# Scheduling a transformer block's instruction queues with the timeline simulator, through an inner tile context

## The chip, the cores and the metric

The kernel runs on one core of a Trainium2 chip. The metric is the device time of one execution in microseconds (us), as the slowest core shows it; a median over several executions is quoted with its range.

The profile of this kernel shows five queues of instructions that run side by side (their busy times in the kernel before add up to 1612.7 us in a span of 740.6 us) and wait for each other by semaphores (the longest wait of TensorE there, for VectorE, took 2.6 us): TensorE (PE in the profile; PEld is its weight load), VectorE (DVE), ScalarE (ACT), GpSimd (POOL) and the sync engine (SP), which here issues nearly all transfers (298 of 322). Each queue has an order, and it counts: in copy_late, one of the runs below, one copy stands five places further back on VectorE, and TensorE waited 2.4 us for it. The text of a kernel does not fix these orders: a scheduler in the tile layer does when the program is built, except where the kernel asks for program order.

## The reference, cut to what matters

```python
def _A_ref(x, wqkv, wo):                     # x: 1 x 2048 x 1024 in bf16, 32 heads of 32
    q, k, v = split(x @ wqkv)
    phi = lambda t: jnp.where(t > 0, t + 1, jnp.exp(t)) + 1e-6
    pq, pk = phi(q), phi(k)
    kv = jnp.einsum("bhsd,bhse->bhde", pk, v);  z = jnp.einsum("bhsd->bhd", pk)
    num = jnp.einsum("bhqd,bhde->bhqe", pq, kv)
    den = jnp.einsum("bhqd,bhd->bhq", pq, z)[..., None] + 1e-6
    return merge_heads(num / den) @ wo
def _B_ref(x, W_gate, W_up, W_down):          # 1024 -> 3584 -> 1024
    gate = x @ W_gate;  gate = gate * (gate > 0)
    return (gate * (x @ W_up)) @ W_down
h = x + _A_ref(_layernorm(x), wqkv, wo)
h2 = h + _B_ref(_layernorm(h), W_gate, W_up, W_down)
```

## The kernel before

The large products are done with Strassen's scheme: seven products of half size (tags A, D, E) instead of eight, and sums of inputs and of weights on VectorE. In time the kernel is: a start (layer norm of the first tiles, transposition on TensorE, plain K and V products), Strassen products for K and V, Strassen products for Q, the attention output in 16 tiles of 128 tokens, an early part of the gated MLP, then the MLP, where the kernel itself fixes the order of TensorE, VectorE and ScalarE, and the down projection.

*The start.* A token tile is transposed on TensorE into a PSUM tile `tp`, of which there is one buffer (`bufs=1`). So TensorE can't begin the next four transposes before the copy out of `tp` is done (in the trace of after, one copy ended at 26.67 us and the transposes behind it began at 26.73), on VectorE for the first half of a tile and on ScalarE for the second.

```python
        def ln_T(t):                                            # cut
            for k in range(2):
                nc.vector.bn_stats(out=stats[:, k, :], in_=x_sb[:, k * NW:(k + 1) * NW])      # L256
            nc.vector.bn_aggr(out=mv[:], in_=stats[:])                                        # L258
            ...
        def transpose_in(t, xn):
            s, i, r = place(t)
            for k in range(2):
                pt = pspool.tile([P, KH, P], BF16, tag="D", bufs=1, name="tp")
                for kc in range(KH):
                    nc.tensor.transpose(pt[:, kc, :], xn[:, (k * KH + kc) * P:(k * KH + kc + 1) * P], ident[:])   # L283
                (nc.scalar.copy if k else nc.vector.tensor_copy)(                             # L284
                    out=xT[s][i][:, k * KH:(k + 1) * KH, r:r + P], in_=pt[:])
```

*The attention output.* A tile goes through a chain: products `nd` on TensorE (L511), logarithm and exponential on ScalarE (L515, L517), a multiplication on VectorE (`o_sb`, L518), a transposing transfer (`oT`, L525), the output product on TensorE (`attn`, L541, 16 matmuls), the residual sum on VectorE (`x_res`, L543). `nd` and `attn` share three PSUM buffers. The kernel traces half of the 224 Q products (L438) among the first tiles, and the early MLP products (L705) among the later ones.

```python
    rest = [p for s in range(1, NS) for c in range(0, KH, 2) for p in [q_unit(s, c)] * 6]
    for step in range(QSTEPS):
        now = rest[step * len(rest) // QSTEPS:(step + 1) * len(rest) // QSTEPS]
        ...
        attn_step(step)
        ...
        for p in now:
            next(p)
```

*The loads of the down projection's weights*, in the MLP, on the sync queue. Sums of W_down (`wt`) are stored to `t_dram` through the same queue.

```python
            if k == nwin - 3:
                for x in range(2):
                    t = wpools[1].tile([P, KC * 2 * GP * P], BF16, tag=("wg", "wu")[x], name="wd")
                    wtiles[x] = t[:, 0:FQ * DW].rearrange("p (f d) -> p f d", f=FQ)
                    load_w(0, x)                                # L837, 896 KB each
```

## Time and profile before

| | before |
|---|---|
| time, median | 744.03 us (743.5 to 746.0, 3 runs) |
| span of the profiled run | 740.6 us |
| TensorE busy, granted clock | 721.8 us, 1.00 |

The first lines are the page's parts 1 and 2: busy time by engine, and the span in 40 equal slices, where a digit is the busy share, or for PEclk the granted clock, in tenths (9 is 90% or more).

```profile
span 740.6 us, 10570 instructions
PE 721.8 (97%) x3967; PEld 382.0 (52%) x4020; DVE 563.2 (76%) x991; ACT 322.0 (43%) x580; POOL 5.7 (1%) x44
...
PE   7999999999989999999999999999999999999997
...
PEclk9999999999999999999999999999999999999999
```

TensorE is what bounds this kernel: 18.8 us of the span without it busy is all there is to win by order.

The same by stretches of time (windows view of before; columns: window, length, then busy us of PE, PEld, DVE, ACT, POOL with instructions in brackets, PEclk as a fraction, DMA share, GB/s).

```profile
core 0: us, PE busy (x) PEld busy (x) DVE busy (x) ACT busy (x) POOL busy (x), PEclk, DMA share, GB/s
20.00:40.00 20.00, 19.89 (x98) 9.28 (x99) 19.45 (x48) 16.11 (x33) 0.00 (x0) 1.00 0.74 154
...
190.00:260.00 70.00, 65.62 (x346) 31.38 (x351) 57.48 (x153) 50.10 (x137) 0.31 (x1) 1.00 0.74 170
```

In the attention stretch TensorE has 4.4 us of idle time in 70.

What TensorE waited for (waits view of before: engine, what waited, what released it; us in total, times, longest), first the longest in 0 to 60 us, then those of 1 us and more in 180 to 260 us:

```profile
PE tp L283 <- DVE xT L284: 2.6, 1, 2.6
```

```profile
PE Eq L705 <- DVE hs L117: 2.0, 1, 2.0
PE Aq L438 <- ACT u L154: 1.1, 1, 1.1
PE nd L511 <- DVE o_sb L518: 1.0, 2, 0.8
```

The order can be read from TensorE's timeline of before in the attention stretch (start, us, then the group of matmuls, and in square brackets the idle time just before it):

```profile
186.28 1.46 PE L438 MATMUL Aq<-xT,tq 128*128 128x512 bf16 x5 [1.10 <-ACT u L154]
187.57 3.62 PE L541 MATMUL attn<-wo_mem,oT 128*128 128x512 bf16 x16
191.03 0.59 PE L438 MATMUL Aq<-xT,tq 128*128 128x512 bf16 x2
191.46 1.89 PE L438 MATMUL Eq<-xS,wq_sb 128*128 128x512 f16 x8
193.18 0.63 PE L511 MATMUL nd<-kvz,pq_mem 128*128 128x132 bf16 x8
193.65 1.03 PE L705 MATMUL Aq<-hn,wg 128*128 128x512 bf16 x4
```

Output products (L541), Q products (L438), `nd` (L511) and early MLP products (L705) alternate, and nothing waits but 1.10 us. (A matmul of 512 columns starts every 216 ns: 16 in 3.45 us.)

### The profile page before, as it was taken

Reading aid. Unit: us, or ns where it says so; the run is one execution under the profiler, and the core shown is the slowest. Engines: PE = TensorE matmul, PEld = TensorE weight load, DVE = VectorE, ACT = ScalarE, POOL = GpSimd, SP = SyncE. Lnnn points to the kernel's source line nnn. Section 1 sums busy time; section 2 is a strip of 40 time slices with the busy share of each in tenths; the row PEclk is TensorE's granted clock in tenths of the full one; section 3 lists DMA queues with packets and bytes.
Section 4 is the critical chain, followed back from the end, with each engine's and each line's share of the span. In section 5 each row is a group of like instructions: output and inputs, shape, how many; then the busy total and the mean of one; then the engine's idle time right before and its main releaser. Section 6 shows DMA issues by size and latency. Waiting matters only on the chain.

```text
span 740.6 us, 10570 instructions
## 1 busy us (share of the span) xinstructions
PE 721.8 (97%) x3967; PEld 382.0 (52%) x4020; DVE 563.2 (76%) x991; ACT 322.0 (43%) x580; POOL 5.7 (1%) x44
## 2 busy tenths in 40 slices
PE   7999999999989999999999999999999999999997
PEld 3444555444444444444444444444444458888666
DVE  6997653675887767778778777877787479996797
ACT  4786553778686654444344434443435120000000
POOL 0000000000000000000000000000000000000000
PEclk9999999999999999999999999999999999999999
DMA  9765003079797526164638359475483399988822
GB/s 319 167 140 157 0 1 107 9 155 242 152 223 165 138 73 203 46 181 137 196 127 233 109 181 288 162 221 201 170 271 127 124 396 345 326 286 298 300 79 79
DMA packets 146579, 132.03 MB, mean 178 GB/s; under 512 B 50912, under 2 KB 128096, under 8 KB 146528
## 3 DMA queue, kind: packets, MB, share of 16 engines
q1 hardware_dynamic: 135392, 123.23, 55.3%
q10 hardware_dynamic: 11136, 8.13, 3.4%
q8 instruction: 31, 0.51, 0.3%
q14 instruction: 20, 0.16, 0.1%
HBM read 79.95 MB, written 39.85 MB: 162 GB/s over the span
## 4 chain that ended last, share of the span: by engine, by line
PE 78%; DVE 8%; ACT 7%; DMA 5%; issue 2%; SPq 0%; DVEq 0%; POOL 0%; ACTq 0%
PE accA L785 22%; PE accX L785 8%; PE accY L785 8%; PE accA L1117 8%; PE Aq L298 3%; PE accA L946 3%; PE accX L1117 3%; PE Aq L438 3%; DMA hn<-hn 2%; PE accY L1117 2%; PE attn L541 2%; PE Aq L705 2%; PE Eq L298 2%; PE accY L946 2%; PE accX L946 2%
## 5 line engine op out<-in xcount | busy, mean ns | idle before, releaser
L795 ACT ACTIVATE gu<-gu 128x512 bf16<-128x512 bf16 x72 | 45.4, 631 | 131.5 <-DVE gu L794 131.5
L790 ACT COPY snap<-accA 128x1024 f32<-128x1024 f32 x72 | 72.5, 1008 | 36.3 <-PE accA L785 36.2
L785 PEld LDWEIGHTS <-tg 128*128 128x128 f16 x384 | 37.6, 98 | 45.3
L785 PEld LDWEIGHTS <-tu 128*128 128x128 f16 x384 | 37.6, 98 | 45.3
L541 PE MATMUL attn<-wo_mem,oT 128*128 128x512 bf16 x249 | 57.9, 379 | 1.2 <-DVE o_sb L518 0.4
L794 DVE TENSOR_TENSOR gu<-accY,snap 128x1024 bf16<-128x1024 f32 x36 | 43.9, 1219 | 10.0 <-ACT snap L790 10.0
L785 PE MATMUL accA<-hn,tu 128*128 128x512 f16 (+1 forms) x192 | 49.3, 379 | 0.0
L785 PE MATMUL accA<-hn,tg 128*128 128x512 f16 (+1 forms) x192 | 49.3, 379 | 0.0
L794 DVE TENSOR_TENSOR gu<-accX,snap 128x1024 bf16<-128x1024 f32 x36 | 43.9, 1219 | 6.2 <-PE accX L785 3.7
L154 ACT COPY u<-Aq 128x512 f32<-128x512 f32 x56 | 32.4, 582 | 37.3 <-PE Aq L298 19.3
L1117 PEld LDWEIGHTS <-x 128*128 128x128 f16 (+1 forms) x448 | 43.8, 98 | 5.5
L785 PEld LDWEIGHTS <-wg 128*128 128x128 bf16 x288 | 28.2, 98 | 34.0
L785 PEld LDWEIGHTS <-wu 128*128 128x128 bf16 x288 | 28.2, 98 | 34.0
L541 PEld LDWEIGHTS <-oT 128*128 128x128 bf16 x256 | 24.6, 98 | 30.8 <-issue 2.9
L798 DVE TENSOR_TENSOR hq<-gu 128x512 bf16<-128x512 bf16 x48 | 20.3, 423 | 14.3 <-ACT gu L795 14.2
L298 PEld LDWEIGHTS <-xT 128*128 128x128 bf16 (+1 forms) x192 | 18.6, 98 | 23.7 <-issue 2.3
L1117 PEld LDWEIGHTS <-xs 128*128 128x128 f16 x280 | 27.4, 98 | 3.2
L543 DVE SCALAR_TENSOR_TENSOR x_res<-attn,x_res 128x512 bf16<-128x512 f32 x32 | 21.8, 687 | 7.2 <-PE attn L541 7.1
L946 PEld LDWEIGHTS <-x 128*128 128x128 bf16 (+1 forms) x168 | 16.4, 98 | 19.6
L518 DVE TENSOR_TENSOR o_sb<-nd,rd 128x384 bf16<-128x384 f32 (+1 forms) x48 | 22.8, 507 | 4.5 <-ACT rd L517 4.4
L1123 DVE TENSOR_TENSOR snap<-accA,u 128x1024 f32<-128x1024 f32 x16 | 19.5, 1220 | 8.3 <-PE accA L1117 8.0
L785 PE MATMUL accA<-hn,wu 128*128 128x512 bf16 x96 | 24.6, 379 | 0.0
(232 smaller groups left out, 1400.8 us busy)
## 6 DMA issues: line engine op xcount, KB each, us to landing
x<-x_dram SPq DMA_DIRECT2D x17, 896.0 KB, 8.2
x_dram<-hq SPq DMA_DIRECT2D x28, 512.0 KB, 3.1
wg<-in_B_W_gate_dram SPq DMA_DIRECT2D x14, 512.0 KB, 5.2
wu<-in_B_W_up_dram SPq DMA_DIRECT2D x14, 512.0 KB, 7.3
wraw<-in_B_W_down_dram SPq DMA_DIRECT2D x14, 512.0 KB, 4.8
x_dram<-hq SPq DMA_DIRECT2D x28, 256.0 KB, 2.6
t_dram<-wt SPq DMA_DIRECT2D x28, 256.0 KB, 2.2
xd<-x_dram SPq DMA_DIRECT2D x6, 896.0 KB, 7.1
```

The costliest lines, as they stand in the source:

```text
L154: nc.scalar.copy(out=snaps[nm, v], in_=A[v][:])
L298: nc.tensor.matmul(ps[:], lhsT=left[m - 1][:, kc, r + v * P:r + (v + 1) * P], rhs=right[m - 1][:, kc, :], start=(start and kc == 0), stop= ...
L438: nc.tensor.matmul(ps[:], lhsT=rq[m - 1][:, kc, (c + v) * P:(c + v + 1) * P], rhs=left[m - 1][:, kc, :], start=(start and kc == 0), stop=( ...
L518: nc.vector.tensor_tensor(out=ov[:, c0:c0 + n], in0=ndv[:, :, 0:P].rearrange("p k (h e) -> p k h e", h=HPC), in1=rd[:, 0:n, :].unsqueeze(3 ...
L541: nc.tensor.matmul(ps[:], lhsT=st["oT"][:, c, :], rhs=wo_sb[:, c, j * NW:(j + 1) * NW], start=(c == 0), stop=(c == KC - 1))
L543: nc.vector.scalar_tensor_tensor(out=h_sb[:, j * NW:(j + 1) * NW], in0=ps[:], scalar=1.0, in1=h_sb[:, j * NW:(j + 1) * NW], op0=ALU.mult, ...
L785: nc.tensor.matmul(ps[:, v, :], lhsT=w[v][n - 1][:, kc, :], rhs=left[n - 1][:, kc, :], start=(t is not None and kc == 0), stop=(kc == KH - ...
L790: nc.scalar.copy(out=st[nm][:], in_=halves(st["A"]))
L794: add(out=g[:], in0=halves(st[nm]), in1=st[base][:], op=ALU.add)
L795: nc.scalar.activation(out=g[:, 0, :], in_=g[:, 0, :], func=ACT.Relu)
L946: nc.tensor.matmul(ps[:, t * NW:(t + 1) * NW], lhsT=x_tile(n, s, kh)[:, f, (t0 + t) * P:(t0 + t + 1) * P], rhs=w_tile(n, kh)[:, f, :], sta ...
L1117: nc.tensor.matmul(pv[:, tt, :], lhsT=left(m)[:, f, tt * P:(tt + 1) * P], rhs=right(m)[:, f, :], start=(t is not None and f == 0 and tt % ...
```

## The change

The body is put into an inner tile context, which is scheduled with a timeline simulator instead of with the default scheduler. The intent is an order in which fewer instructions wait. No instruction of the body is added, removed or resized.

```diff
-    block_kernel(tc, A_x, A_wqkv, A_wo, B_W_gate, B_W_up, B_W_down, out, H=32)
+    with tc.tile_critical(), tile.TileContext(tc.nc, schedule_with_timeline_sim=True) as inner:
+        block_kernel(inner, A_x, A_wqkv, A_wo, B_W_gate, B_W_up, B_W_down, out, H=32)
```

The built programs show what it does: on every engine the same instructions in another order up to the MLP. From there on TensorE, VectorE and ScalarE have the same order (the kernel fixes it), and only the sync queue differs, by a few places.

## The prediction

> **What bounds the kernel now.** TensorE: busy 721.8 of 740.6 us (the profile's first part), granted clock 1.00 in all windows, 16 matmuls of 512 columns in 3.45 us in the chain of waits (216 ns each). It idles only 19 us, by windows: 0-20 us, 4.2 (1.2 for the zeroed tile, 2.6 for the first transposed tile's copy); 20-155 us, 2.3; 155-225 us (last Q units, attention output), 5.0; 225-291 us, 2.1; 291-727 us (the gated MLP), 1.4; tail, 4.3. With start and tail fixed, about 10 us at most can be won.
>
> **What the change does.** The built programs have the same matmuls, vector, scalar and DMA instructions; they are permuted. A nested entry and exit add a branch and a semaphore hand-over per engine at the start, and a barrier and some waits at the end. Before, the gap between the constants and the first real instruction is about 0.3 us; I estimate 0.5 to 2 us for all of it.
>
> From 291 us on the program fixes the order of TensorE, VectorE and ScalarE by hand, the same in both. Only the sync queue differs there, by a few places (weight loads against stores). TensorE idles 1.2 us in 291-578, so loads come early enough: nothing expected.
>
> The first 291 us are reordered, more finely: independent Strassen products and single kv matmuls sit between dependent ones (the K unit's second product starts during the V tiles). In 20-155 us that saves at most the 2.3 us, mostly where VectorE is full (20.0 of 20 us in 40-60). The start's first copy still queues behind the second tile's statistics: no gain.
>
> **The doubtful stretch is attention output.** The old order mixes five of sixteen attention tiles with Q products. The new one finishes Q earlier and runs seven tiles back to back, then three more with ten other matmuls between. A tile costs TensorE 16 x 216 + 8 x 58 ns = 3.9 us; ScalarE, by that window's groups, three log/exp pairs (1.4), square with read-out (1.3), normalise (1.24), three small ones (0.7) = 4.7 us. DMA already shows 1.03 of capacity in 155-195. So ten tiles take ScalarE about 47 us against 41 for TensorE: about 6 us idle, plus DMA latency (transposes land in 3.4 us), partly offset by earlier first transposes. [...] TensorE idles 2.0 us on one vector sum at 218 us.
>
> **Sum.** Entry and exit +1; 20-155 us -1; attention stretch +4; early MLP products 0: **748 us**, range 742 to 757. Faster by over 2%: 0.02; within 2%: 0.87; slower: 0.11.
>
> **What would show it.** Right: TensorE busy time unchanged; 9 to 15 us idle instead of 7 from the first attention tile to the hand-ordered part, with ScalarE above 90% or DMA at 1.0; at most 2 us idle between 20 us and the Q units; the hand-ordered part 436 us as before. Wrong: idle in the hand-ordered part (the sync queue mattered), or less idle in the attention stretch (earlier transposes paid).
>
> **What would make it wrong.** One badly placed in-order wait (a load behind a waiting store, a matmul ahead of a late transpose) costs several us and repeats with the tiles; or the finer interleaving hides nearly all waits, giving about 738.

Its sum: 744.0 + 1 - 1 + 4 + 0 = 748 us. The +1 for entry and exit is the estimate; the only figure of the trace behind it is the gap of 0.3 us.

## The result, and the profile after

| | before | after |
|---|---|---|
| time, median (range), fast runs | 744.71 us (743.5 to 746.0, 4 runs) | 777.21 us (776.08 to 777.37, 4 runs) |
| ratio (95% interval) | | 1.0433 (1.0411 to 1.0455): slower |
| span of the profiled run | 740.6 us | 774.3 us |
| TensorE busy, rest of the span | 721.8, 18.8 us | 729.7, 44.6 us |

A ratio here is the mean time of one kernel's fast runs over that of the other's of the same rounds, so it is not quite the ratio of the quoted medians. Executions over 1.5% slower than the fastest of the same kernel are left out of the means. (The medians of before differ a little between tables, as each set of runs has its own runs of before.)

The page, parts 1 and 2, of after:

```profile
span 774.3 us, 10590 instructions
PE 729.7 (94%) x3967; PEld 384.6 (50%) x4020; DVE 565.1 (73%) x991; ACT 322.5 (42%) x580; POOL 5.0 (1%) x44
...
PE   7698999998786999999999999999989999999997
...
PEclk9899999999999999999999999999999999999999
```

TensorE has the same matmuls and is busy 7.9 us longer, and idle 25.8 us longer. The holes are in slices 2 and 11 to 13.

**Where the time goes.** Because the matmuls are the same, the two traces can be compared at equal work: count for each moment the matmul work done so far (each matmul with its duration at full clock, groups with missing records scaled up to their known count), and take the time at which after has done as much, minus the time at which before had. This lag is worked out from the start times of the matmuls; it is not a view of the profile. Two executions of equal order differ in it by up to about 3 us (start_from_after, below, which is in before's order by then, goes from 8.6 us at 170 us of work to 11.2 at 290), in steps that come with single pieces of lowered clock (nest_only: some 2.5 us near 225 us). The profiled run of before has no such piece until its end (granted clock 1.00), while most other runs of before show 0.994 to 0.998. So a lag against it is a little too long, and what a part costs is better taken from the times.

```
work done, us              10     15     20     40    100    170    190    210    290    520    560    716
before has it at, us     15.7   21.2   26.4   47.6  109.0  180.5  202.1  226.4  309.0  539.3  579.5  735.3
lag of after              3.0   11.1   11.1   10.0   11.7   10.1   23.4   28.9   28.0   27.8   32.0   32.1
lag of flag_only          3.5   10.6   10.4    9.4   10.8   10.3   22.6   28.4   27.1   27.1   30.8   31.0
```

(flag_only is the second kernel of the experiments: after's order without the nesting.) So there are three places, and next to nothing in between: the start (up to 32 us in after's trace), the attention output (190 to 255 us), and one spot in the MLP (near 575 us).

**The start.** Windows view of after, to be read against the same columns of before:

```profile
20.00:32.00 12.00, 5.70 (x25) 2.69 (x24) 12.00 (x30) 5.26 (x13) 0.00 (x0) 0.72 0.18 52
...
190.00:260.00 70.00, 52.14 (x263) 24.40 (x266) 41.18 (x115) 40.18 (x119) 0.71 (x4) 0.93 0.78 182
```

In 20 to 32 us VectorE is busy without a gap and TensorE for 5.70 us of 12, at a mean clock of 0.72. The longest entry of TensorE's waits in 0 to 60 us of after:

```profile
PE tp L283 <- DVE xT L284: 9.9, 3, 6.3
```

The wait of 2.6 us for the first copy is there as before; two more have come, the longest of 6.3 us, for the third tile's copy. VectorE's timeline of after shows what stood ahead of that copy:

```profile
18.91 1.21 DVE L133 TENSOR_TENSOR tv<-wv_sb 128x2048 f16<-128x2048 bf16 x1
...
20.11 2.46 DVE L256 BATCH_NORM_STATS2 stats<-x_sb 128x6 f32<-128x512 bf16 x4
22.49 1.20 DVE L134 TENSOR_TENSOR tv<-wv_sb,tv 128x2048 f16<-128x2048 bf16 x1
23.62 2.46 DVE L256 BATCH_NORM_STATS2 stats<-x_sb 128x6 f32<-128x512 bf16 x4
...
26.26 0.41 DVE L284 COPY xT<-tp 128x512 bf16<-128x512 bf16 x1
```

Two sums for the V weights and the statistics of four later tiles, 7.3 us, none of it needed soon. In before the same copy stands behind one weight sum (VectorE's timeline of before):

```profile
16.18 1.17 DVE L134 TENSOR_TENSOR pq_mem<-pq_mem 128x2048 f16<-128x2048 bf16 x1
17.27 0.42 DVE L284 COPY xT<-tp 128x512 bf16<-128x512 bf16 x1
```

In after, TensorE had finished the transposes by 20.4 us and started the next ones at 26.73:

```profile
20.05 0.39 PE L283 MATMUL tp<-ident,xn 128*128 128x128 bf16 x4
26.73 0.58 PE L283 MATMUL tp<-ident,xn 128*128 128x128 bf16 x4 [6.30 <-DVE xT L284]
27.11 3.62 PE L331 MATMUL kp<-pq_mem,xT 128*128 128x512 bf16 x8
```

The last line shows a second cost: 8 matmuls in 3.6 us, where before did 16 in 3.8. Here the granted clock has dropped to one half, as it did at five places in this trace after waits, in pieces of 3.413 us, here two in a row (427 ns from one matmul's start to the next, not 216). So the start's 11 us are 7.3 us more waiting and up to 4.0 us of half clock (the clock was lowered from 10.9 to 14.3 and from 24.5 to 31.4 us, and TensorE was busy for 8.0 us of that).

**The attention output.** Waits of TensorE in 180 to 260 us of after:

```profile
PE attn L541 <- DMA oT<-o_sb: 8.3, 3, 4.8
PE nd L511 <- DVE x_res L543: 3.7, 4, 2.3
PE attn L541 <- DVE o_sb L518: 2.5, 3, 1.5
PE nd L511 <- DVE o_sb L518: 2.2, 1, 2.2
```

Every link of the tile's own chain appears. TensorE's timeline of after shows why:

```profile
202.28 3.61 PE L541 MATMUL attn<-wo_mem,oT 128*128 128x512 bf16 x16 [0.44 <-DVE o_sb L518]
205.74 0.51 PE L511 MATMUL nd<-kvz,pq_mem 128*128 128x132 bf16 x6
206.69 0.28 PE L511 MATMUL nd<-kvz,pq_mem 128*128 128x132 bf16 x2 [0.44 <-DVE x_res L543]
207.46 3.61 PE L541 MATMUL attn<-wo_mem,oT 128*128 128x512 bf16 x15 [0.49 <-DVE o_sb L518]
210.91 0.51 PE L511 MATMUL nd<-kvz,pq_mem 128*128 128x132 bf16 x6
216.19 5.04 PE L541 MATMUL attn<-wo_mem,oT 128*128 128x512 bf16 x16 [4.76 <-DMA oT<-o_sb]
```

There is nothing but output and `nd` products: the Q products are used up. Counted in the built programs:

```
Q products (of 224) still to come when output tile 1, 2, 3, 4, 5, 6 starts
before    71  59  48  43  10   0
after     24   0   0   0   0   0
```

And neither ScalarE nor the transfers are full there: ScalarE is busy 40.18 of 70 us in the window above, less than before's 50.10, and the DMA share is 0.78. The loss between 190 and 260 us is 13.5 us more idle time (17.9 against 4.4 us) and up to 4.6 us of half clock (mean 0.93). The place in the sync queue has a part too: in the longest wait the tile's `o_sb` was done at 208.96 us, but its transfer was issued at 210.81, behind another transposing transfer, a store and a weight load, and landed at 216.14. No run tests that part alone.

**The MLP.** Between 520 and 600 us TensorE waits for nothing in before. The longest entry in after:

```profile
PE accX L785 <- DVE gu L794: 3.0, 1, 3.0
```

VectorE in turn stands still for 7.06 us, ahead of a weight sum (timeline of after):

```profile
576.37 0.69 DVE L650 TENSOR_TENSOR wt<-wraw 128x1024 f16<-128x1024 bf16 x1 [7.06 <-issue]
```

"issue" says that the profile names no releaser. The transfers do: `wt` has one buffer, and its last store has to land first (it landed at 576.19 us, the sum starts at 576.37). From the records of the sync queue's issues (worked out from the trace, times in us):

```
before   537.36 wd load, 896 KB    landed 542.94          after   565.14 wd load, 896 KB    landed 570.76
         538.22 t_dram <- wt       landed 544.13 (5.92)           566.01 wd load, 896 KB    landed 574.09
         540.53 wd load, 896 KB    landed 548.57                  566.73 t_dram <- wt       landed 576.19 (9.46)
```

In after the two loads are issued back to back, ahead of the store. The store, issued behind both loads, landed after both and took 9.46 us instead of 5.92.

### The profile page after: what moved, and what is told of

It is laid out like the page before. It is cut to its first block, busy times and chain, and to the rows that moved or that the text cites. A ratio compares the mean times of both kernels' runs of the same rounds, so it can differ in the third digit from the quotient of the medians.

```text
span 774.3 us, 10590 instructions
## 1 busy us (share of the span) xinstructions
PE 729.7 (94%) x3967; PEld 384.6 (50%) x4020; DVE 565.1 (73%) x991; ACT 322.5 (42%) x580; POOL 5.0 (1%) x44
## 4 chain that ended last, share of the span: by engine, by line
PE 82%; DMA 6%; DVE 6%; ACT 2%; issue 2%; SPq 0%; POOL 0%; DVEq 0%; ACTq 0%
PE accA L785 20%; PE accA L1117 8%; PE accX L785 8%; PE accY L785 7%; PE attn L541 7%; PE Aq L705 4%; PE Aq L298 3%; PE Aq L438 3%; PE accA L946 3%; PE accX L1117 3%; DMA xT<-xn 3%; PE accY L1117 2%; PE Eq L705 2%; DMA oT<-o_sb 2%; PE Eq L298 2%
## 5 line engine op out<-in xcount | busy, mean ns | idle before, releaser
L541 PE MATMUL attn<-wo_mem,oT 128*128 128x512 bf16 x249 | 62.4, 401 | 11.1 <-DMA oT<-o_sb 8.3
L785 PE MATMUL accA<-hs,tg 128*128 128x512 f16 x96 | 24.6, 379 | 0.0
```

The lines of the kernel that those rows point to most:

```text
L541: nc.tensor.matmul(ps[:], lhsT=st["oT"][:, c, :], rhs=wo_sb[:, c, j * NW:(j + 1) * NW], start=(c == 0), stop=(c == KC - 1))
L785: nc.tensor.matmul(ps[:, v, :], lhsT=w[v][n - 1][:, kc, :], rhs=left[n - 1][:, kc, :], start=(t is not None and kc == 0), stop=(kc == KH - ...
```

## The experiments

Theory A: the new order costs, at the three places. Rival B: the nesting costs. Later theories are named where they come up. Kernels that share a set of runs share the runs of before.

### 1 and 2: the nesting alone, and the flag alone

```diff
 nest_only: the inner context, default scheduling
+    with tc.tile_critical(), tile.TileContext(tc.nc) as inner:
+        block_kernel(inner, ...)
 flag_only: no inner context, the flag on the outer one
-    with _tile.TileContext(nc) as tc:
+    with _tile.TileContext(nc, schedule_with_timeline_sim=True) as tc:
```

The build shows that the first has exactly before's order on all engines, and the second exactly after's.

> The nested context without the timeline scheduler; every engine's order is that of before. Theory A (the order costs all but the entry and exit): 745 to 747 us, the span 1.5 to 2 us longer than before, lag constant from the first matmul on. Rival B (the nested context slows the DMA queue, whose issues take 0.6 us in the changed kernel's trace against 0.4 us before): 755 us or more, with the longer issues.

> The timeline scheduler on the outer context, no nesting; every engine's order is that of the changed kernel. Theory A: 774 to 776 us, with the same three stretches of lost time (about 11 us by the start's end, 17 us in attention output, 4 us near the end of the gated MLP). Rival B: 745 to 765 us.

| | time, us | ratio (95%) |
|---|---|---|
| before | 744.37 (742.92 to 746.13) | |
| nest_only | 748.55 (747.73 to 749.15) | 1.0051 (1.0027 to 1.0075) |
| flag_only | 772.46 (771.10 to 773.79) | 1.0376 (1.0350 to 1.0402) |

The order makes some 28 of the 32 us, the nesting some 4. Rival B falls as the main cause. Theory A's direction holds, but both times lie outside its ranges, because the nesting costs about twice what it allowed. In the profile of nest_only 1.7 us arise in the first 10 us, some 2.5 us near 225 us, with one piece of lowered clock, and 1.6 us after the last of the work. The piece of lowered clock is not the nesting's: the runs of before in the same rounds have a mean granted clock of 0.997 as well. The longer issues that rival B named are real: a transfer's issue on the sync queue takes 602 ns (median) in nest_only, 422 in before and 423 in flag_only. But with them the kernel is only some 4 us slower.

### 3 and 4: two local edits with the scheduler left free

In the changed kernel, start_fix holds back the V sums and the statistics of later tiles with order edges; mix asks for program order of TensorE in the Q and attention loop, so that Q products and tiles alternate as traced.

```diff
 start_fix
+            with behind():          # behind the last VectorE copy out of tp, once there is one
+                ln_T_now(t)
-                v_sums()
+                with behind():
+                    v_sums()
 mix, around the loop over QSTEPS
+    mixctx.enter_context(tc.manual_schedule(engines={mybir.EngineType.PE}))
```

> The changed kernel, but VectorE may not take up the V weight sums and the statistics of later tiles before the last copy that TensorE's transposes wait for. Theory A (work put ahead in VectorE's queue holds those copies back): the 6.3 us wait at the start goes, the lag at the end of the start falls from 11 us to 1 to 4 us, and the time to 767 to 771 us. Rival C (VectorE has too much to do at the start in any order, so the wait comes back later): 774 us or more.

> The changed kernel, but TensorE keeps program order in the loop that mixes attention tiles with Q products, so attention tiles stand between Q pieces again; the rest is left to the scheduler. Theory A (attention tiles back to back have nothing that fills the time of their chain through ScalarE, VectorE and the transposing DMA): the loss from the first attention tile to the hand-ordered part falls from 17 us to 8 us or less, the time to 761 to 768 us. Rival D (my prediction: ScalarE or DMA is full in this stretch, so mixing only moves the wait): the loss stays above 13 us, 773 us or more.

Both missed: 785.10 us (783.25 to 785.44, ratio 1.0541) and 788.85 us (787.91 to 789.75, ratio 1.0596), slower than the changed kernel. In start_fix the waits for copies fell to 5.7 us, but V products then waited 5.4 us for VectorE, and the lag was 20 us at 50 us of work instead of 12. In mix the attention stretch lost some 30 us instead of 18. The built programs told why these runs prove little: the scheduler placed much else anew. Counted by instruction, 199 of 959 VectorE places, 215 of 588 of ScalarE and 50 of 298 of the sync queue differ from after in mix, and 79, 45 and 4 in start_fix. One thing mix does show: when its first five output tiles start, 80, 72, 56, 48 and 24 Q products are still to come, about as in before, and yet the stretch loses more. So Q products between the tiles on TensorE are not enough by themselves. An edit is only an experiment if the rest stands still.

### How the other experiments hold the rest still

They start from the kernel before (no nesting) and pin every queue, instruction by instruction, to a given list with edges that only order and wait for nothing:

```diff
+def _pin(tc, nc, mybir):
+    traced = {i.name: i for i in nc.cur_bb.bb.instructions}
+    for numbers in ORDER:                       # one list per engine, numbers of traced instructions
+        queue = [f"I-{n}" for n in numbers]
+        for before, later in zip(queue, queue[1:]):
+            tc.add_manual_dep(traced[later], before,
+                              mybir.DependencyInfo(mybir.DependencyClass.NoSync, mybir.DependencyReason.DATA),
+                              reason="pinned order")
     with _tile.TileContext(nc) as tc:
         tile_sequential_...(tc, *args)
+        _pin(tc, nc, _mybir)
```

Pinned to before's lists, the build gives before's order in every place, and pinned to after's lists, that of after. A piece of one order can so be put into the other. A list that no execution could follow shows itself as a deadlock when it is built.

### 5 to 8: one stretch at a time

- start_from_after: all that after schedules ahead of its first V product, in after's order; then the rest in before's.
- attn_from_after: before's order up to its first Q product; then after's up to the MLP; then before's.
- copies_first: after's order, but in the start VectorE's copies and K steps stand ahead of V sums and later statistics (31 VectorE and 15 ScalarE places).
- wd_apart_flat: after's order, but on the sync queue, six places:

```diff
 sync queue
   load wd (first)
-  load wd (second)
   store t_dram3 <- wt
-  load xd
   store x_dram1_1 <- hq (a)
+  load wd (second)
+  store x_dram1_1 <- hq (b)
   store t_dram0 <- wt
-  store x_dram1_1 <- hq (b)
   store t_dram1 <- wt
+  load xd
```

> The kernel before (no nesting, default scheduling), with every engine's queue pinned by order-only edges: first all the instructions that the changed kernel schedules ahead of its first V product, in the changed kernel's order, then all the others in the order of before. Theory A (the order of the start costs 10 to 11 us and nothing after it gives that back): 753 to 757 us; the lag behind before is +9 to +11 us by 32 us of matmul work and stays there to the end; the wait of the second xT copy on VectorE (6.3 us) is there. Rival C (what is lost in the start is work moved ahead of time, which comes back later as work already done): the lag falls again by more than 4 us in the next 100 us, and the time is below 750 us.

> The kernel before with its own order up to its first Q product, then the changed kernel's order for all that is left ahead of the gated MLP (Q products, attention output, early MLP products), then before's order again. Theory A (the order within the Q and attention stretch makes the loss there): 760 to 764 us, no lag up to 150 us of work, +15 to +19 us after the attention output, and none added in the MLP. Rival D (the loss comes from what the changed kernel did in the K and V part, so it needs the earlier order too): below 752 us.

> The changed kernel's order on all engines (without the nesting; the run of that order took 772.5 us), with one edit, in the start: on VectorE and ScalarE the copies of the transposed tiles and the K map's steps stand ahead of the V weight sums and of the statistics of later tiles, which follow in their own order (31 places on VectorE, 15 on ScalarE, none on TensorE). Theory A (that place in those two queues is what makes the start's lag): the lag at 32 us of work falls from +10.4 to +1 to +4 us, and the time to 763 to 767 us. Rival C (the delayed statistics make a wait of about the same length a little later, as in the run that let the scheduler place everything else again): the lag is back at +9 us or more by 60 us of work, and the time is 770 us or more.

> The changed kernel's order on all engines (without the nesting; 772.5 us), but on the sync queue the seven issues around the first two wd loads stand as in before: the second wd load goes behind the store of the last weight sums and two other issues (6 places differ, no other engine). Theory A (the two loads back to back delay that store, and with it VectorE and TensorE): the rise of 3.7 to 4.2 us near 570 us is gone, and the time is 768 to 769.5 us; the store lands in under 6.5 us and not in 9.5. Rival E (the rise comes from the order of the arithmetic engines, which is unchanged here): 772 to 773 us.

| | time, us | ratio (95%) | lag at 32, 170, 290, 716 us of work |
|---|---|---|---|
| before | 743.33 (741.94 to 745.65) | | |
| start_from_after | 753.29 (751.92 to 753.69) | 1.0132 (1.0107 to 1.0156) | 10.1, 8.6, 11.2, 11.2 |
| attn_from_after | 758.22 (757.73 to 759.09) | 1.0199 (1.0172 to 1.0226) | 0.0, -1.4, 16.8, 16.6 |
| copies_first | 773.59 (772.22 to 775.25) | 1.0409 (1.0380 to 1.0438) | 13.0, 11.9, 28.0, 30.1 |
| wd_apart_flat | 768.52 (766.53 to 769.02) | 1.0335 (1.0308 to 1.0361) | 10.1, 8.5, 24.3, 24.1 |

The start alone costs 10 us and nothing gives it back; the attention stretch alone costs 15 us in time, 18 in the profile's lag (-1.4 to 16.8); the MLP's step is gone with six places of the sync queue (lag 24.09 at 520 and at 560 us of work, where flag_only went from 27.1 to 30.8), and the store takes 5.82 us instead of 9.4. The time, 768.52 us, lies in the range that theory A gave; by the ratios it fell by 0.4% of before, 3 us.

copies_first missed theory A's range, as start_fix had, and came out as rival C said (773.59 us, lag 13.8 us at 60 us of work). The copy is in time now, but the V products wait instead (waits of TensorE in 0 to 120 us):

```profile
PE vp L349 <- DVE wo_mem L336: 7.3, 1, 7.3
PE tp L283 <- DVE xT L284: 5.3, 3, 2.7
```

The block of V sums and statistics had only been moved from ahead of one step of VectorE that TensorE waits for to ahead of another.

### 9 and 10: which queue's order costs in the start

In start_da only VectorE and ScalarE have after's order within the start (100 and 34 places), and TensorE is exactly before's. start_pe was meant as the counterpart, with after's order on TensorE alone (49 places). The built program shows that it isn't: everything that after does ahead of its first V product was put ahead of the rest on VectorE and ScalarE too, and there 70 and 17 places differ from before.

> As the run that took the start from the changed kernel and the rest from before (753.3 us), but within the start only TensorE has the changed kernel's order (49 places differ); VectorE and ScalarE keep before's order there. Theory A1 (the start's +10 us comes from the places on VectorE and ScalarE): at most +3 us of lag at 32 us of work, 743 to 747.5 us. Theory A2 (it comes from TensorE's order, which puts whole tiles of transposes behind each other and leaves nothing between a copy and the next transpose): +8 us or more, 751 to 755 us.

> The counterpart: within the start only VectorE and ScalarE have the changed kernel's order (100 and 34 places), TensorE keeps before's. Theory A1: +7 us or more of lag at 32 us of work, 750 to 756 us. Theory A2: at most +3 us, 743 to 747.5 us. If both this run and its counterpart show 4 us or more, the two orders cost only together or each by itself, and neither theory stands.

start_pe took 756.48 us (754.91 to 759.18, ratio 1.0172), start_da 755.11 us (754.97 to 757.03, ratio 1.0158), before in the same rounds 743.89 us (741.78 to 745.37). The longest wait of TensorE in each, in 0 to 90 us, first start_pe, then start_da:

```profile
PE vp L349 <- DVE wo_mem L336: 9.8, 1, 9.8
```

```profile
PE tp L283 <- DVE xT L284: 10.6, 3, 5.7
```

start_da fits theory A1 (750 to 756 us): after's order on VectorE and ScalarE is enough to cost the whole of the start, with a lag of 14.1 us at 20 us of work already. Its longest wait, 5.7 us, is again for the third tile's copy, behind the same V sums and statistics.

start_pe says little about TensorE's order. At 20 us of work, while VectorE still works in before's order, its lag is 2.5 us. The other 11 us come with the wait of 9.8 us for a K step that has been pushed behind 11.9 us of statistics, V sums and an input sum (from 27.03 us on), one of the 70 places (VectorE's timeline of start_pe):

```profile
34.72 1.18 DVE L133 TENSOR_TENSOR tv<-wv_sb 128x2048 f16<-128x2048 bf16 x1
...
38.94 0.68 DVE L336 SCALAR_TENSOR_TENSOR wo_mem<-kp,e 128x512 bf16<-128x512 f32 x1
```

So theory A2 isn't shown, and what TensorE's order would cost beyond these 2.5 us, with VectorE left alone, stays open. In both runs the loss is the same block of work ahead of a step that TensorE needs. VectorE is busy for 19.45 of the 20 us from 20 to 40 us in before and for 19.57 in after, so there is little slack for such a block.

### 11 and 12: the Q products as filling

q_early is before with the 71 Q products that are left at the first output tile, and their finishing steps, moved ahead of that tile. q_late is after's order with the last 71 taken out and put back in five pieces behind the first five output tiles; 16 weight sums of the early MLP had to go behind them, since they need the memory that the Q products free.

```diff
 q_early, TensorE (VectorE and ScalarE accordingly)
+  Q products x71
   attn tile 1
-  Q products x12
   attn tile 2
-  Q products x11, ...
```

> The kernel before with all queues pinned to its own order, with one edit: the 71 Q products still to come when the first output-projection tile starts (of 224), with the VectorE and ScalarE steps that finish them, are moved up ahead of that tile. Nothing is added. Theory F (Q products are what fills TensorE while an attention tile goes through logarithm, exponential, multiplication and transposing transfer; without them the tiles stand bare): +8 to +14 us, all of it between 180 and 250 us of work, 752 to 758 us. Rival G (the stretch loses in the changed kernel because of the places on VectorE and the other queues, and early Q products alone do no harm): below 747.5 us.

> The changed kernel's order on all engines (without the nesting; 772.5 us), with one edit in the attention stretch: the last 71 Q products with their finishing steps are taken out and put back in five pieces of 14 or 15, one behind each of the first five output-projection tiles; the 16 weight sums of the early MLP, which need the memory that the Q products free, go behind the last piece. Theory F: the loss between 180 and 250 us of work falls from 17 us to 4 to 10 us, and the time to 758 to 766 us. Rival G: at most 4 us are won, 768 us or more.

q_early took 761.47 us (761.24 to 763.0, ratio 1.0239): 17.6 us lost by moving 71 products with the steps that finish them (54 places on VectorE, 64 on ScalarE), with no work added, more than the 8 to 14 expected. The lag is 0 up to 150 us of work and 19.2 at 290: the whole loss of the changed kernel in this stretch (18). The waits, in 180 to 290 us of q_early, are again the links of the tiles' chain:

```profile
PE attn L541 <- DVE o_sb L518: 8.2, 5, 4.9
PE nd L511 <- DVE x_res L543: 2.2, 5, 0.4
```

q_late missed: 784.49 us (783.14 to 785.43, ratio 1.0543), slower than the order it was to mend. Its lag grows by 6 us at 150 us of work already, and TensorE waits 7.2 us for one `o_sb`. The 47 of these products that stood ahead of the first output tile had been filling there, and their steps on VectorE and ScalarE, put back in lumps, stand ahead of the tiles'. So filling taken from one place is missed in that place; where it has to go can't be chosen for one queue by hand without the others. What of the 12 us (1.7% of before) belongs to the lumps and what to the missing filling is open. With mix, it is the second run that gives Q products back between the tiles and does not win: that Q products are needed there is shown in before's order (q_early), that they would be enough in after's is not.

### 13 to 16: what was still open

- attn_from_before: after's order up to its first Q product, then before's.
- sums_late: after's order, with only the 16 early weight sums moved behind on VectorE.
- copy_late: before, the third tile's copy on VectorE five places back. copy_early: before, the first tile's copy three places ahead.

```diff
 copy_late, VectorE                        copy_early, VectorE
-  copy xT <- tp   (third tile)           +  copy xT <- tp   (first tile)
   min e; nmr; K sum; max k; min e           statistics x2, aggregate (second tile)
+  copy xT <- tp   (third tile)           -  copy xT <- tp   (first tile)
```

> The changed kernel's order on every queue up to its first Q product, then before's order for all that is left. Theory F (the loss in the attention stretch is made by the order within that stretch): the lag is that of the start, 9 to 11 us, and hardly grows after it (at most +3 us); 752 to 757 us. Rival D (the changed kernel's K and V part leads to the loss): +10 us or more are lost after 180 us of work, 760 us or more.

> The changed kernel's order (without the nesting; 772.5 us), with the 16 weight sums of the early MLP moved behind on VectorE, behind the sixth output-projection tile begins, and nothing else (no other engine's order differs). Rival G (these sums, 16 times 0.41 us, stand in front of the steps of the attention tiles and cause a good part of the loss): 4 us or more are won, 768.5 us or less. Theory F: the tiles wait on their own chain of steps, so 2 us at most are won, 770.5 to 773 us.

> The kernel before with one instruction moved: on VectorE the third tile's copy of transposed values stands five places (2.5 us of work by the trace) further back; TensorE, ScalarE and the sync queue are unchanged. Theory H (VectorE is full there and TensorE has nothing else, so what stands in front of a copy is paid in full, and a lowered clock can come on top): +2 to +5 us, lag made at 20 us of work and kept, 746 to 749 us. Rival I (there is slack between the copies, and it takes more than one misplacement): at most +1 us.

> The kernel before with one instruction moved: on VectorE the first tile's copy of transposed values stands ahead of the second tile's two statistics and their aggregation, which wait for a load; the 2.56 us wait of TensorE for it should shrink to under 1 us. Theory H: 0.5 to 2.1 us less than before (741.5 to 743.5 us), unless the first K products then wait for their weights. Rival I: no change (within 0.5 us). This is also the attempt at a version faster than both.

| | time, us | ratio (95%) | lag at 32, 170, 290, 716 us of work |
|---|---|---|---|
| before | 744.09 (742.08 to 745.0) | | |
| attn_from_before | 754.48 (752.86 to 755.06) | 1.0138 (1.0118 to 1.0159) | 11.4, 11.7, 11.6, 11.6 |
| sums_late | 768.03 (766.56 to 768.69) | 1.0322 (1.0304 to 1.0340) | 10.6, 9.5, 22.1, 24.2 |
| copy_late | 746.47 (745.18 to 747.72) | 1.0035 (1.0016 to 1.0053) | 3.4, 3.1, 5.3, 5.3 |
| copy_early | 744.83 (744.32 to 746.04) | 1.0015 (1.0001 to 1.0029) | 0.7, 0.6, 3.0, 3.0 |

attn_from_before loses nothing in the attention stretch: the changed kernel's K and V part is not to blame, and rival D falls. sums_late wins about 4 us against flag_only's ratio (1.0376): the weight sums ahead of the tiles' steps on VectorE have a share, as rival G said, though in its profile 12.6 us of the 16.8 stay. copy_late pays for one copy 2.5 us too late with 3.4 us of lag (some 2.6 us by the ratio): a wait of 2.4 us and one piece of half clock. VectorE did not work ahead of its queue here, and TensorE's transposes waited 2.4 us for the late copy. copy_early took the 2.56 us wait away (waits of TensorE in 0 to 90 us of copy_early),

```profile
PE kp L331 <- DMA pq_mem<-in_A_wqkv_dram: 0.9, 1, 0.9
...
PE tp L283 <- DVE xT L284: 0.5, 1, 0.5
```

but the K products then wait for their weights, as its expectation allowed, and nothing is won. No version run here beats before.

## Why the prediction was right or wrong

The prediction was 748.0 us with a range to 757; the result is 777.2. It saw rightly that TensorE bounds the kernel with some 10 us at most to be won, that the order alone changes, that the doubtful stretch is the attention output with its bare tiles, and, under what would make it wrong, that one badly placed wait costs several us (6.3 us for one copy in after). It failed in four terms of its sum, of which the first two make most of the 29 us.

1. **"attention stretch +4"** was the step that failed most. It measured 15 us by time and 18 by lag (attn_from_after). The mechanism was wrong: it took the tiles' throughput on ScalarE ("ten tiles take ScalarE about 47 us against 41 for TensorE") and awaited ScalarE above 90% or DMA at 1.0. ScalarE was busy 57% there and DMA at 0.78. What limits a bare tile here is the length of its chain, with three PSUM buffers to run ahead in (in after, TensorE waited 16.7 us for its links between 180 and 260 us). q_early shows it in before's order: 71 Q products moved, no work added, 17.6 us. About 4 us are the share of the weight sums ahead on VectorE (sums_late). That filling given back would mend after's order is not shown (mix and q_late lost more).
2. **"20-155 us -1", and for the start "no gain".** The prediction looked at the first copy in the start, which did stay as it was (2.57 us), and not at the third, which now stood behind 7.3 us of VectorE work for later. It treated the full VectorE as something that finer interleaving relieves. Measured: +10 us (start_from_after), and the order of VectorE and ScalarE alone is enough for it (start_da, 755.11 us).
3. **"nothing expected" for the hand-ordered MLP.** It argued from the small idle time of TensorE there that the loads come early enough. They do; what came late was a store behind two of them (9.46 us to land), and the weight sum waiting for its buffer. Measured: 3.7 us of lag, 3 us by time (wd_apart_flat). Its own sign for this, idle time in the hand-ordered part, was the right one.
4. **"Entry and exit +1"** measured about 4 us (nest_only): the term was right in kind and too small, with 1.7 us at the start and 1.6 at the end in the profile; where the small rest arises is open.

"TensorE busy time unchanged" failed too: +7.9 us, because the clock was lowered after waits (the pieces of half clock in after's trace hold 17.2 us of busy TensorE, so up to 8.6 us are lost in them). No term of the sum had allowed for that.

The parts add up within their spread: 10 for the start, 15 for the attention stretch, 3 for the MLP and 4 for the nesting make 32 us, and 32.5 were measured. Open remains why the simulator puts the V sums and the Q products as early as it does; no run here looked into it.

## What to carry to other kernels

Two orders of the same instructions differ by what stands ahead of the one instruction that the bounding engine waits for: look, queue by queue, at what comes ahead of each copy out of a single buffer, and count how much independent work is left when a chain with little buffering begins. Throughput of the helpers didn't tell that here (ScalarE was busy 57% where 18 us were lost); latency and filling did. To test an order, pin all queues and move one thing: a local hint to a scheduler moves much else too, and so can a cut between two orders, as in start_pe. So compare the built orders of all queues with the original before reading the time.

## What the traces show of the clock and of the stores

- The clock. In the trace of after it was granted at one half from 10.87 to 14.29 us, from 24.53 to 31.35, 195.19 to 198.61, 215.67 to 219.09, 242.98 to 246.39 and from 772.05 us to the end: pieces of 3.413 us, the second time two in a row, in which a matmul of 512 columns started every 427 ns instead of 216. Such a piece cost up to 1.7 us where TensorE was busy all through it. The length of a single wait does not tell whether one follows: waits of 2.15 us (copy_early, attention stretch), 2.22 us (nest_only) and 2.57 us (after, for the first copy) were each followed by such a piece, and waits of 2.00 and 2.56 us in before were not. Worked out from the clock records and TensorE's busy time: in the 3.413 us right ahead of the six lowered stretches of after, TensorE was idle for 62%, 100%, 92%, 100%, 73% and 96%, so not all of them lay behind a stretch without any work. These six start whole multiples of 3.413 us after one another (4, 50, 6, 8 and 155 of them). With both traces cut into stretches of that length, counted from a lowered piece, a stretch that was not followed by half clock had at most 58% of idle time in after and 49% in before, where these two waits were each cut in two (32% and 43% of two stretches; 49% and 32%). That is what these two traces show; what decides in general is not shown.
- The stores. A store of 256 KB (`t_dram`) took 9.46 us in after, behind two loads of 896 KB on one queue (9.37 and 7.74 in flag_only and sums_late), and 5.92 in before, behind one. The median of the 28 such stores was 2.2 us in before and 2.4 us in after.
